# The angle of the last layer in turns, and 64-row expert blocks whose halves TensorE adds

## The chip, the cores and the metric

The kernel runs on one core of a Trainium2 chip. The metric is the device time of one execution in microseconds (us). TensorE is called PE here, its weight loads PEld, VectorE DVE, ScalarE ACT, GpSimd POOL, and SyncE, which issues most transfers, SP.

## What is computed

Three layers run one after another: attention over pooled queries, eight experts of which each routed row uses one, and a last dense layer with a cosine. The parts that the change touches are these two.

```python
for e in range(E):                                   # experts, 512 -> 1024 -> 512
    mask = e_idx == e
    h = np.maximum(xc[mask] @ w1[e], 0.0)
    y[mask] = gate_w[mask, None] * (h @ w2[e])
out[do_compute] = xc + y

h = x @ w_in                                         # last layer, 512 -> 2048 -> 512
g = h * np.cos(h)
return (g @ w_out).astype(np.float32)
```

Here x has 2304 rows. The inputs are float32, and w_out is float64 (the kernel sees it as pairs of 32-bit words).

## The kernel before

A scheduler takes the program as written and sets the order of the instructions on each engine by its own estimates; each engine then runs its queue in order. So an edit can reorder work that it does not touch.

**Split operands.** Every large product is made of three: a float32 operand is split into a rounded part and the rest (names ending in h and l), and high by high, high by low and low by high are summed in PSUM.

**Experts** (about 553 to 748 us). The rows are handled in 13 blocks of 256, 128 or 64 rows; eight of the 13 have 64. The weights come in pieces: SP issues a load into one of six buffers (stage, L696), ACT rounds it (whl, L701), and DVE makes the rest (L702). For a block of 64 rows, the input's two parts stand side by side as 128 columns, so one product gives the partial sum of the high part in PSUM partitions 0 to 63 and that of the low part in 64 to 127. mm1's function hidden adds the two: for each of two halves of 512 columns, DVE copies the lower partitions up (L747) and adds the upper ones (L748). The result hs (64 x 1024) is turned by eight 64 x 64 transposes on PE (L677 in transposed), and then ACT applies Relu and rounds (L680) and DVE makes the rest (L681). Then the second product (ops), DVE's y with gate and residual (L791, L793) and POOL's scatter to HBM follow. ORDERS gives the order in which pieces of a block's first product, the block before's second product and the transposes are written.

**Last layer** (class Ffn, from about 751 us to the end). The rows come in six chunks of 384, in three pairs, and there are 16 column steps f for each pair. A step has 24 matmuls into hp (12 for each chunk, L955) and 18 into o (9 for each chunk, L984); the o products of a chunk run five items of work (LAG) behind its hp products. While the first pair runs, the weights of each step are loaded and split too: wih and wil (L909 to L911) from wraw, and w_out in narrow(), where four DVE operations and one ACT square build float32 numbers from 64-bit words (woo, L875 to L882), then woh (L920, mostly POOL) and wol (L921, mostly DVE). Pairs two and three find the weights ready.

**The angle.** With sin² of half the angle, h·cos(h) is −2·h·(sin²−½). For each chunk and step, ACT computes t = hp/2π + MAGIC, whose addition rounds to a whole number (L958), and copies hp to h (L959). POOL takes MAGIC off again and multiplies by −C1 (L960), DVE adds h (L961), and DVE adds the small rest of 2π (L962). ACT takes the sine of half of that and squares it (L966, L967), DVE makes h = (r − ½)·h (L968), POOL rounds it (gh, L970), and DVE or POOL makes the rest (gl, L971; by the table GLP, POOL makes 11 of the first pair's 32). The factor −2 is applied to the output (L1031, L1033).

Of the kernel before, what the change touches and what calls it, by code (L numbers as in the profile page):

```python
# [634 lines left out]
class Experts:  # L635
    def __init__(self, tc, ctx, stage, early, xts, w1, w2, ident, xg, x2, lst):
        self.tc, self.nc, self.ident = tc, tc.nc, ident
        self.w1, self.w2, self.xg, self.x2, self.lst = w1, w2, xg, x2, lst
        pool = lambda name, bufs, **kw: ctx.enter_context(tc.tile_pool(name=name, bufs=bufs, **kw))
        self.stage, self.early, self.count = stage, early, 0  # L640

        self.hl0 = pool("hl0", 1)
        self.px = pool("ex1", 2)
        self.hl1 = pool("hl1", 1)
        self.p2 = pool("ex2", 2)
        self.p3 = pool("ex3", 6)
        self.psh = pool("psh", 2, space=PSUM)
        self.pst = pool("pst2", 2, space=PSUM)
        self.pso = pool("pso", 2, space=PSUM)
        self.prev, self.xts = [], xts  # L650

    def gather(self, off, rows):
        nc = self.nc
# [7 lines left out]
    def transposed(self, srcs, nch, rows, relu=False):  # L661


        nc = self.nc
        part = lambda t: (self.px if nch == 4 else self.p2).tile([128, nch, 256], F32R, name=("xT" if nch == 4 else "hT") + t, bufs=2)
        if rows == 64:
            both = part("h")
            tiles = [(both[:, :, 0:64], both[:, :, 64:128], nch)]
        else:
            both = part("h"), part("l")  # L670
            tiles = [tuple(t[:, :, 128 * b:128 * b + 128] for t in both) + (4,) for b in range(len(srcs))]
        for src, (hi, lo, n) in zip(srcs, tiles):
            for c0 in range(0, nch, n):
                tp = self.pst.tile([128, n, min(rows, 128)], F32, name="tp2")
                for c in range(n):
                    m = tp.shape[2]
                    nc.tensor.transpose(tp[:, c, :], src[0:m, (c0 + c) * 128:(c0 + c + 1) * 128], self.ident[0:m, 0:m])  # L677
                h, l = hi[:, c0:c0 + n], lo[:, c0:c0 + n]
                if relu:
                    nc.scalar.activation(h, tp, AF.Relu)  # L680
                    nc.vector.scalar_tensor_tensor(l, tp, 0.0, h.bitcast(F32), ALU.max, ALU.subtract)  # L681
                else:
                    nc.scalar.copy(h, tp)
                    nc.vector.tensor_tensor(l, tp, h.bitcast(F32), ALU.subtract)
        return both
# [26 lines left out]
    def mm1(self, group, xT, rows):  # L712
# [20 lines left out]
        def hidden():  # L733
            if rows == 256:
                hh, hl = (self.p2.tile([128, 8, 256], F32R, name="hT" + t, bufs=2) for t in "hl")
                for a in range(4):
                    p = h[a // 2][:, a % 2, :].rearrange("p (a b) -> p a b", a=2)
                    s = slice(2 * a, 2 * a + 2)
                    nc.scalar.activation(hh[:, s], p, AF.Relu)
                    nc.vector.scalar_tensor_tensor(hl[:, s], p, 0.0, hh[:, s].bitcast(F32), ALU.max, ALU.subtract)  # L740
                res.append((hh, hl))
                return
            hs = self.p2.tile([128, FF], F32, name="hs")
            for a in range(2):
                s = slice(512 * a, 512 * a + 512)
                if rows == 64:
                    nc.vector.tensor_copy(hs[0:64, s], h[0][64:128, a, :])  # L747
                    nc.vector.tensor_tensor(hs[0:64, s], h[0][0:64, a, :], hs[0:64, s], ALU.add)  # L748
                else:
                    nc.scalar.activation(hs[:, s], h[0][:, a, :], AF.Relu)  # L750
            res.append(hs)
# [134 lines left out]
class Ffn:  # L886

    MAGIC = 12582912.0
    C1 = 6.28125
    C2 = 0.0019353071795864769  # L890

    def __init__(self, tc, ctx, w_in, w_out64, ident, x2, out):
        self.tc, self.nc, self.ident, self.x2, self.out = tc, tc.nc, ident, x2, out
# [52 lines left out]
    def hidden(self, x, f, m):  # L946
# [8 lines left out]
                nc.tensor.matmul(hp, w[:, d], a[:, d], start=d + k == 0, stop=d == 3 and k == 2)  # L955
        T = lambda name, dt=F32, bufs=3: self.p3.tile([128, 384], dt, name=name, bufs=bufs)
        t, r, h = T("t", F32, TB), T("r", F32, RB), T("h", F32, HB)
        nc.scalar.activation(t, hp, AF.Identity, bias=self.magic, scale=0.15915494309189535)  # L958
        self.copied = nc.scalar.copy(h, hp)  # L959
        nc.gpsimd.tensor_scalar(t, t, -self.MAGIC, -self.C1, ALU.add, ALU.mult)  # L960
        nc.vector.tensor_tensor(r, t, h, ALU.add)  # L961
        nc.vector.scalar_tensor_tensor(r, t, self.C2 / self.C1, r, ALU.mult, ALU.add)  # L962

        def rest():
            with self.tc.issue_after(self.copied.ins):
                nc.scalar.activation(r, r, AF.Sin, scale=0.5)  # L966
                nc.scalar.activation(r, r, AF.Square)  # L967
                nc.vector.scalar_tensor_tensor(h, r, 0.5, h, ALU.subtract, ALU.mult)  # L968
                gh, gl = T("gh", F32R, LAG + 1), T("gl", F32R, LAG + 1)
# [16 lines left out]
    def run(self):  # L986
# [35 lines left out]
        def project():  # L1022
# [4 lines left out]
            if f == 15:  # L1027
                for t in range(3):
                    ot = self.p1.tile([128, DM], F32, name="fx", bufs=6)
                    if t == 1:  # L1030
                        nc.vector.tensor_scalar(ot, o[m][t], -2.0, 0.0, ALU.mult, ALU.add)  # L1031
                    else:
                        nc.scalar.mul(ot, o[m][t], -2.0)  # L1033
                    nc.sync.dma_start(self.out[384 * m + 128 * t:384 * m + 128 * t + 128, :], ot)

        for f in range(WO):
# [168 lines left out]
```

## Time and profile before

| | us |
|---|---|
| three runs | 1192.21, 1194.04, 1196.78 |
| median | 1194.04 |
| the profiled execution, its own time | 1202.32 |
| its span, first to last instruction | 1200.6 |

In the profiled execution PE is busy for 93% of the span, DVE for 79%, ACT for 65% and POOL for 49%, and the mean granted clock is 0.979 of full speed. Busy shares are averages over three layers with different limits, so the stretches have to be read one by one. Matmuls overlap, and the record's end of a matmul is modelled: the rate of PE is better read from the start of one group to the start of the next.

### The profile page before, as it was taken

What the parts mean: (1) busy time and instruction counts of PE and PEld (TensorE: products, weight loads), DVE (VectorE), ACT (ScalarE), POOL (GpSimd) and SP (SyncE); (2) the same over time, 40 slices, a digit from 0 to 9 for tenths busy, and PEclk for the clock granted to TensorE, in tenths of its full rate; (3) what the DMA queues carried; (4) which work ended last, traced back from release to release, by engine and by line L of the source; (5) the groups of instructions that cost most, each with busy time, mean ns of one, the idle gap of its engine ahead of it and who ended that gap; (6) DMA issues with size and microseconds to landing.
All of it is one profiled execution on the core that took longest, in us unless ns stands there. A gap on an engine that the chain in (4) does not pass through costs nothing. (4 is left out here: it accounts for less than half of the span.)

```text
span 1200.6 us, 20635 instructions
## 1 busy us (share of the span) xinstructions
PE 1119.4 (93%) x6722; PEld 1002.4 (83%) x6722; DVE 946.3 (79%) x1957; ACT 775.9 (65%) x2016; POOL 584.4 (49%) x828
## 2 busy tenths in 40 slices
PE   3999999999999999999999996789998999999998
PEld 2999898899888999898776874678877989898987
DVE  7989898999898999898689657698987755565554
ACT  3889898899888999897266433554444544454443
POOL 7587666776576666734412121355454332223231
PEclk9999999999999999998999998889998999999999
DMA  6575567466664566343568542532111300010001
GB/s 182 148 197 146 154 201 174 123 162 172 205 175 120 152 202 167 105 136 132 176 207 295 188 179 76 201 115 71 53 53 36 106 1 1 1 53 1 1 1 53
DMA packets 62638, 147.72 MB, mean 123 GB/s; under 512 B 17882, under 2 KB 17882, under 8 KB 62528
## 3 DMA queue, kind: packets, MB, share of 16 engines
q1 hardware_dynamic: 59840, 141.75, 40.1%
q0 software_dynamic: 2688, 4.62, 1.2%
q8 instruction: 55, 0.90, 0.3%
q14 instruction: 55, 0.45, 0.1%
HBM read 91.93 MB, written 21.69 MB: 95 GB/s over the span
## 5 line engine op out<-in xcount | busy, mean ns | idle before, releaser
L234 DVE TENSOR_REDUCE m<-s 128x1 f32<-128x384 f32 x432 | 236.8, 553 | 48.5 <-PE s L225 37.8
L243 ACT ACTIVATE p<-s,m 128x384 f32<-128x384 f32 x432 | 247.8, 583 | 21.6 <-DVE m L238 18.7
L225 PE MATMUL s<-k,qa 128*128 128x384 f32 x768 | 226.9, 379 | 34.1 <-ACT p L243 18.3
L261 PE MATMUL tp<-ident,p 128*128 128x128 f32 x1296 | 202.2, 275 | 5.0 <-DVE ptsml L277 3.2
L261 PEld LDWEIGHTS tp<-ident,p 128*128 128x128 f32 x1296 | 162.6, 142 | 18.0 <-issue 2.1
L225 PEld LDWEIGHTS s<-k,qa 128*128 128x128 f32 x768 | 119.3, 194 | 43.7 <-ACT p L243 25.8
L958 ACT ACTIVATE t<-hp,magic 128x384 f32<-128x384 f32 x96 | 55.6, 579 | 138.5 <-PE hp L955 138.5
L955 PE MATMUL hp<-fxh,wih 128*128 128x384 f32 x384 | 131.6, 343 | 8.4 <-ACT h L959 7.0
L955 PE MATMUL hp<-fxl,wih 128*128 128x384 f32 x384 | 130.3, 339 | 0.5 <-DVE fxl L942 0.5
L955 PE MATMUL hp<-fxh,wil 128*128 128x384 f32 x384 | 130.3, 339 | 0.0
L960 POOL TENSOR_SCALAR t<-t 128x384 f32<-128x384 f32 x96 | 60.5, 630 | 137.0 <-ACT t L958 134.1
L984 PE MATMUL o<-woh,gh 128*128 128x512 f32 x288 | 116.0, 403 | 3.1 <-ACT woh L918 3.1
L984 PE MATMUL o<-wol,gh 128*128 128x512 f32 x288 | 115.7, 402 | 2.0 <-DVE wol L921 2.0
L984 PE MATMUL o<-woh,gl 128*128 128x512 f32 x288 | 115.2, 400 | 0.0
L277 DVE TENSOR_TENSOR ptbigl<-tp,ptbigh 128x384 fp32r<-128x384 f32 x208 | 112.3, 544 | 0.0
L961 DVE TENSOR_TENSOR r<-t,h 128x384 f32<-128x384 f32 x96 | 68.0, 708 | 52.8 <-POOL t L960 52.3
L970 POOL TENSOR_SCALAR gh<-h 128x384 fp32r<-128x384 f32 x96 | 70.4, 746 | 77.3 <-DVE h L968 70.1
L968 DVE SCALAR_TENSOR_TENSOR h<-r,h 128x384 f32<-128x384 f32 x96 | 56.4, 622 | 58.3 <-ACT r L967 58.3
L701 ACT CAST whl<-stage 128x1024 fp32r<-128x1024 f32 x64 | 66.2, 1054 | 55.5 <-DMA stage<-w 39.8
L272 ACT CAST ptbigh<-tp 128x384 fp32r<-128x384 f32 x208 | 93.9, 491 | 10.2 <-PE tp L261 9.5
L277 DVE TENSOR_TENSOR ptsml<-tp,ptsmh 128x384 fp32r<-128x384 f32 x176 | 95.2, 546 | 1.5 <-ACT ptsmh L272 1.5
L272 ACT CAST ptsmh<-tp 128x384 fp32r<-128x384 f32 x176 | 81.4, 489 | 20.9 <-PE tp L261 14.6
(237 smaller groups left out, 2860.6 us busy)
## 6 DMA issues: line engine op xcount, KB each, us to landing
stage<-w SPq DMA_DIRECT2D x64, 512.0 KB
k<-stage SPq DMA_DIRECT2D x60, 288.0 KB
qa<-stage SPq DMA_DIRECT2D x60, 256.0 KB
stage<-v SPq DMA_DIRECT2D x16, 576.0 KB
stage<-q SPq DMA_DIRECT2D x15, 576.0 KB
stage<-k SPq DMA_DIRECT2D x15, 576.0 KB
wiw<-w_in SPq DMA_DIRECT2D x16, 512.0 KB
wow<-w_out SPq DMA_DIRECT2D x16, 512.0 KB
```

What stands on the lines that cost most here:

```text
L225: nc.tensor.matmul(o[:, 0:384], w, m[:, 384 * n:384 * n + 384], start=t == 0, stop=t == len(prods) - 1)
L234: self.last_max = nc.vector.tensor_reduce(s["m", c][:, n:n + 1], s["s", c, n][:, 0:384], AX.X, ALU.min)
L243: self.nc.scalar.activation(s["p", c][:, 384 * n:384 * n + 384], s["s", c, n][:, 0:384], AF.Exp, bias=s["m", c][:, 3:4], scale=-1.0, accum ...
L261: nc.tensor.transpose(tp[:, a, :], p[:, (3 * n + a) * 128:(3 * n + a + 1) * 128], self.ident)
L272: self.nc.scalar.copy(hi, tp)
L277: self.nc.vector.tensor_tensor(lo, tp, hi.bitcast(F32), ALU.subtract)
L701: nc.scalar.copy(hi, raw)
L955: nc.tensor.matmul(hp, w[:, d], a[:, d], start=d + k == 0, stop=d == 3 and k == 2)
L960: nc.gpsimd.tensor_scalar(t, t, -self.MAGIC, -self.C1, ALU.add, ALU.mult)
L961: nc.vector.tensor_tensor(r, t, h, ALU.add)
L970: nc.gpsimd.tensor_scalar(gh, h, 1.0, 0.0, ALU.mult, ALU.add)
L984: self.nc.tensor.matmul(o[t], a[:, s], w, start=f + k == 0, stop=f == 15 and k == 2)
```

## The change

In the experts, for blocks of 64 rows, ACT now copies hs whole, all 128 partitions, and the eight transposes become eight products of a 128 x 128 slice of hs with fold, a 128 x 64 tile of two identities one above the other; such a product turns the slice and adds its halves at once. fold is made by two POOL copies at the start of the experts. DVE's copies and additions go. In the last layer, the copy h is hp/2π, so the angle is counted in turns: one DVE operation forms (t − MAGIC) − h, POOL's operation on t and DVE's addition go, the sine's scale is π, and the output's factor is −4π.

```diff
--- before.py
+++ after.py
@@ -648,6 +648,9 @@
         self.pst = pool("pst2", 2, space=PSUM)
         self.pso = pool("pso", 2, space=PSUM)
         self.prev, self.xts = [], xts
+        self.fold = self.px.tile([128, 64], F32, name="fold", bufs=1)
+        for r in (slice(0, 64), slice(64, 128)):
+            self.nc.gpsimd.tensor_copy(self.fold[r], ident[r, r])
 
     def gather(self, off, rows):
         nc = self.nc
@@ -673,8 +676,12 @@
             for c0 in range(0, nch, n):
                 tp = self.pst.tile([128, n, min(rows, 128)], F32, name="tp2")
                 for c in range(n):
-                    m = tp.shape[2]
-                    nc.tensor.transpose(tp[:, c, :], src[0:m, (c0 + c) * 128:(c0 + c + 1) * 128], self.ident[0:m, 0:m])
+                    s, m = slice((c0 + c) * 128, (c0 + c + 1) * 128), tp.shape[2]
+                    if relu:
+
+                        nc.tensor.matmul(tp[:, c, :], src[:, s], self.fold, start=True, stop=True)
+                    else:
+                        nc.tensor.transpose(tp[:, c, :], src[0:m, s], self.ident[0:m, 0:m])
                 h, l = hi[:, c0:c0 + n], lo[:, c0:c0 + n]
                 if relu:
                     nc.scalar.activation(h, tp, AF.Relu)
@@ -744,8 +751,7 @@
             for a in range(2):
                 s = slice(512 * a, 512 * a + 512)
                 if rows == 64:
-                    nc.vector.tensor_copy(hs[0:64, s], h[0][64:128, a, :])
-                    nc.vector.tensor_tensor(hs[0:64, s], h[0][0:64, a, :], hs[0:64, s], ALU.add)
+                    nc.scalar.copy(hs[:, s], h[0][:, a, :])
                 else:
                     nc.scalar.activation(hs[:, s], h[0][:, a, :], AF.Relu)
             res.append(hs)
@@ -886,8 +892,7 @@
 class Ffn:
 
     MAGIC = 12582912.0
-    C1 = 6.28125
-    C2 = 0.0019353071795864769
+    TURN = 0.15915494309189535
 
     def __init__(self, tc, ctx, w_in, w_out64, ident, x2, out):
         self.tc, self.nc, self.ident, self.x2, self.out = tc, tc.nc, ident, x2, out
@@ -955,15 +960,13 @@
                 nc.tensor.matmul(hp, w[:, d], a[:, d], start=d + k == 0, stop=d == 3 and k == 2)
         T = lambda name, dt=F32, bufs=3: self.p3.tile([128, 384], dt, name=name, bufs=bufs)
         t, r, h = T("t", F32, TB), T("r", F32, RB), T("h", F32, HB)
-        nc.scalar.activation(t, hp, AF.Identity, bias=self.magic, scale=0.15915494309189535)
-        self.copied = nc.scalar.copy(h, hp)
-        nc.gpsimd.tensor_scalar(t, t, -self.MAGIC, -self.C1, ALU.add, ALU.mult)
-        nc.vector.tensor_tensor(r, t, h, ALU.add)
-        nc.vector.scalar_tensor_tensor(r, t, self.C2 / self.C1, r, ALU.mult, ALU.add)
+        nc.scalar.activation(t, hp, AF.Identity, bias=self.magic, scale=self.TURN)
+        self.copied = nc.scalar.mul(h, hp, self.TURN)
+        nc.vector.scalar_tensor_tensor(r, t, self.MAGIC, h, ALU.subtract, ALU.subtract)
 
         def rest():
             with self.tc.issue_after(self.copied.ins):
-                nc.scalar.activation(r, r, AF.Sin, scale=0.5)
+                nc.scalar.activation(r, r, AF.Sin, scale=np.pi)
                 nc.scalar.activation(r, r, AF.Square)
                 nc.vector.scalar_tensor_tensor(h, r, 0.5, h, ALU.subtract, ALU.mult)
                 gh, gl = T("gh", F32R, LAG + 1), T("gl", F32R, LAG + 1)
@@ -1028,9 +1031,9 @@
                 for t in range(3):
                     ot = self.p1.tile([128, DM], F32, name="fx", bufs=6)
                     if t == 1:
-                        nc.vector.tensor_scalar(ot, o[m][t], -2.0, 0.0, ALU.mult, ALU.add)
+                        nc.vector.tensor_scalar(ot, o[m][t], -4 * np.pi, 0.0, ALU.mult, ALU.add)
                     else:
-                        nc.scalar.mul(ot, o[m][t], -2.0)
+                        nc.scalar.mul(ot, o[m][t], -4 * np.pi)
                     nc.sync.dma_start(self.out[384 * m + 128 * t:384 * m + 128 * t + 128, :], ot)
 
         for f in range(WO):
```

The scheduler's order moves with it. On DVE in the first pair of the last layer, one column step reads as follows before; woo and wol are the weights of w_out, r, h and gl belong to the angle.

```order
L921 TENSOR_TENSOR wol_10939<-woo,woh_10938 128x512
L968 SCALAR_TENSOR_TENSOR h<-r,h 128x384 x2
L961 TENSOR_TENSOR r<-t,h 128x384
L971 TENSOR_TENSOR gl<-h,gh 128x384
L962 SCALAR_TENSOR_TENSOR r<-t,r 128x384
L971 TENSOR_TENSOR gl<-h,gh 128x384
L875 TENSOR_SCALAR woo<-wow 128x512
L961 TENSOR_TENSOR r<-t,h 128x384
L876 SCALAR_TENSOR_TENSOR woo<-wow,woo 128x512
L962 SCALAR_TENSOR_TENSOR r<-t,r 128x384
L877 SCALAR_TENSOR_TENSOR woo<-wow,woo 128x512
L882 SCALAR_TENSOR_TENSOR woo<-wow,woo 128x512
```

And now:

```order
L926 TENSOR_TENSOR wol_10928<-woo,woh_10927 128x512
L971 SCALAR_TENSOR_TENSOR h<-r,h 128x384 x2
L965 SCALAR_TENSOR_TENSOR r<-t,h 128x384
L974 TENSOR_TENSOR gl<-h,gh 128x384 x2
L881 TENSOR_SCALAR woo<-wow 128x512
L882 SCALAR_TENSOR_TENSOR woo<-wow,woo 128x512
L965 SCALAR_TENSOR_TENSOR r<-t,h 128x384
L883 SCALAR_TENSOR_TENSOR woo<-wow,woo 128x512
L888 SCALAR_TENSOR_TENSOR woo<-wow,woo 128x512
```

The two additions (L961) are gone, and the single operation of the angle (L965) stands where they stood; here both gl are DVE's before and now.

On ACT, at the end of the experts, the last block's rows read as follows before; whl are weight pieces being rounded, hTh is the Relu of the turned block.

```order
L701 CAST whl_10401<-stage_10399 128x1024
L680 ACTIVATE hTh<-tp_10277 128x8x64
L701 CAST whl_10410<-stage_10408 128x1024
L701 CAST whl_10419<-stage_10417 128x1024
L701 CAST whl_10428<-stage_10426 128x1024
L680 ACTIVATE hTh<-tp_10373 128x8x64
```

And now:

```order
L708 CAST whl_10388<-stage_10386 128x1024
L708 CAST whl_10397<-stage_10395 128x1024
L708 CAST whl_10406<-stage_10404 128x1024
L754 COPY hs<-hps 128x512 x2
L708 CAST whl_10415<-stage_10413 128x1024
L687 ACTIVATE hTh<-tp_10360 128x8x64
```

The two copies of hs stand behind three weight pieces and ahead of the last one.

On PE in the middle of the experts, the turning of a 64-row block (tp) stands among the matmuls of the next block's first product (hps). Before:

```order
L772 MATMUL hps<-whl_8562,xTl 128x512
L677 MATMUL tp_8998<-ident,hs 128x64 x4
L772 MATMUL hps<-whl_8562,xTh 128x512 x2
L772 MATMUL hps<-whl_8562,xTl 128x512
L772 MATMUL hps<-whl_8562,xTh 128x512
L772 MATMUL hps<-whl_8565,xTh 128x512
L677 MATMUL tp_8998<-ident,hs 128x64 x4
```

And now:

```order
L778 MATMUL hps<-whl_8562,xTl 128x512
L778 MATMUL hps<-whl_8562,xTh 128x512 x2
L682 MATMUL tp_8999<-fold,hs 128x64 x8
L778 MATMUL hps<-whl_8562,xTl 128x512
L778 MATMUL hps<-whl_8562,xTh 128x512
L778 MATMUL hps<-whl_8565,xTh 128x512
```

The turning is one piece of eight products instead of two pieces of four, and follows its block's products more closely.

## Rows read from the trace of the kernel before

**Rows 1.** Windows, first pair: stretch, us, busy (count) PE PEld DVE ACT POOL, PEclk

```profile
757.00:780.00 23.00, 19.79 (x108) 17.66 (x108) 17.66 (x29) 15.84 (x34) 10.51 (x11) 1.00 0.57 198
780.00:840.00 60.00, 52.17 (x239) 45.81 (x238) 54.76 (x77) 29.65 (x64) 33.62 (x37) 0.91 0.30 93
840.00:900.00 60.00, 57.09 (x279) 49.18 (x277) 54.57 (x84) 26.72 (x60) 29.65 (x38) 1.00 0.17 53
900.00:920.00 20.00, 14.89 (x66) 12.41 (x66) 17.62 (x26) 8.75 (x20) 11.58 (x14) 0.83 0.17 53
```

**Rows 2.** Windows of one line alone: L955 (hp) above, L984 (o) below

```profile
757.00:920.00 163.00, 78.30 (x396) 70.75 (x396) 0.95 0.28 88
...
757.00:920.00 163.00, 70.26 (x261) 50.78 (x261) 0.95 0.28 88
```

**Rows 3.** Chain that ended last: start us, us, what

```profile
871.63 0.69 DVE woo L882
...
880.68 0.69 DVE woo L882
...
935.79 4.19 PE o L984 x18
939.98 4.16 PE hp L955 x24
```

**Rows 4.** Lines of 640 to 900 by form: busy us, mean ns, idle before

```profile
L962 DVE SCALAR_TENSOR_TENSOR r<-t,r 128x384 f32<-128x384 f32 x29 | 23.8, 819 | 0.0
L960 POOL TENSOR_SCALAR t<-t 128x384 f32<-128x384 f32 x29 | 23.3, 805 | 9.4 <-ACT t L958 7.1 <-POOL gh L970 0.2
L961 DVE TENSOR_TENSOR r<-t,h 128x384 f32<-128x384 f32 x29 | 21.1, 729 | 4.2 <-POOL t L960 4.0
...
L968 DVE SCALAR_TENSOR_TENSOR h<-r,h 128x384 f32<-128x384 f32 x27 | 19.2, 741 | 1.0 <-ACT r L967 1.0
...
L971 DVE TENSOR_TENSOR gl<-h,gh 128x384 fp32r<-128x384 f32 x19 | 15.2, 800 | 0.8 <-POOL gh L970 0.8
...
L876 DVE SCALAR_TENSOR_TENSOR woo<-wow,woo 128x512 int32<-128x512 int32 x14 | 10.7, 761 | 0.1
L882 DVE SCALAR_TENSOR_TENSOR woo<-wow,woo 128x512 f32<-128x512 f32 x14 | 10.0, 711 | 1.0
...
L921 DVE TENSOR_TENSOR wol<-woo,woh 128x512 fp32r<-128x512 f32 x12 | 9.7, 806 | 8.2 <-POOL woh L920 8.2
...
L875 DVE TENSOR_SCALAR woo<-wow 128x512 int32<-128x512 int32 x14 | 8.8, 632 | 0.0
```

**Rows 5.** The same view of 850 to 1201, line L962

```profile
L962 DVE SCALAR_TENSOR_TENSOR r<-t,r 128x384 f32<-128x384 f32 x79 | 50.3, 637 | 1.0
```

**Rows 6.** Waits of PE, 757 to 920: us in total, times, longest us

```profile
PE hp L955 <- ACT h L959: 7.0, 7, 2.7
PE hp L940 <- DVE fxl L942: 3.8, 1, 3.8
```

**Rows 7.** Timeline of the last expert block: start us, us, instruction [idle before]

```profile
735.88 1.05 ACT L701 CAST whl<-stage 128x1024 fp32r<-128x1024 f32 x1 [1.51 <-SPq L1175]
...
737.97 0.46 PE L677 MATMUL tp<-ident,hs 64*128 64x64 f32 x4 [1.51 <-DVE hs L748]
...
740.61 0.80 PE L766 MATMUL ops<-whl,hTh 128*128 128x512 f32 x1 [2.18 <-DVE hTh L681]
```

**Rows 8.** Lines of the whole span by form

```profile
L329 PE MATMUL av<-sel,avs 128*128 128x73 f32 x256 | 36.8, 267 | 0.5 <-ACT avs L306 0.5
...
L747 DVE COPY hs<-hps 64x512 f32<-64x512 f32 x16 | 11.1, 693 | 3.3 <-PE hps L766 2.9
...
L677 PE MATMUL tp<-ident,hs 64*128 64x64 f32 x64 | 7.1, 234 | 2.1 <-DVE hs L748 2.0
...
L750 ACT ACTIVATE hs<-hps 128x512 f32<-128x512 f32 x4 | 2.2, 596 | 3.3 <-PE hps L772 3.3
```

**Rows 9.** Waits of ACT in the experts, 560 to 757

```profile
ACT whl L701 <- DMA stage<-w: 39.8, 19, 9.4
```

## Prediction

> **What bounds the kernel now.** I read the windows first, then the chain of work that ended last, then the lines and waits of the stretches that lose time, and the order of both kernels. The last layer's pairs two and three are at PE's rate: in the chain 24 hp products take 4.16 us and 18 o products 4.19 us, one group right behind the other [rows 3]. So a column step costs PE 8.35 us, 0.173 us for an hp product and 0.233 for an o product. From about 930 us to the end nothing but PE sets the time, and an engine relieved there gives nothing.
>
> The first pair is another matter. Between 757 and 920 us PE did 396 hp and 261 o products [rows 2]; at those rates 68.6 + 60.8 = 129.4 us, and some 4 us more for 30 transposes of inputs. The stretch is 163 us long, so about 29 us of PE's time are lost. I spread them over the stretches by their count of instructions, at 133.4/687 = 0.194 us each (the four add up to 692, as an instruction that crosses a border counts twice) [rows 1]: 780 to 840 has 239, worth 46, and loses 14; 840 to 900 has 279, worth 54, and loses 6; 900 to 920 has 66, worth 13, and loses 7; the first 23 us have 108, worth 21, and lose 2, or nearer 4 since most of those are the cheaper hp products. DVE is what stands over these: it is busy 54.76 and 54.57 of 60 us, more than 90% [rows 1], and the chain runs through its operations, with the same woo operation at 871.63 and 880.68 [rows 3]. A step takes 9.05 us there, 0.70 above PE's 8.35. PE's own waits name ACT's h for 7.0 us in seven waits and fxl, DVE's last of the next pair's inputs, for 3.8 us in one [rows 6]. ACT's h has to wait for a buffer that DVE frees, so both go back to DVE. The granted clock is 0.91 and 0.83 of full speed in the two stretches that wait most, and 1.00 in the others [rows 1].
>
> In the experts PE waits little but at the end: in the last block the second half of the transposes starts after 1.51 us of waiting for DVE's addition, and the second product after 2.18 us of waiting for DVE's rest of the Relu [rows 7].
>
> **The angle.** Per chunk and step, one POOL operation and one DVE addition go; of 96 each, 32 lie in the first pair, two a step. The DVE step in the order before has wol, two h, two additions (L961), two L962, two gl, and four woo. By the means of the stretch that is 0.81 + 1.48 + 1.46 + 1.64 + 1.60 + four times about 0.70 = 9.8 us [rows 4]. The step itself took 9.05, so the means, which take in the slow start, are 7% high. Without the additions it is 9.8 − 1.46 = 8.3, or 7.7 scaled by 9.05/9.8. I take 7.7, from the later step, and keep 8.3 for the range; the single operation that stays is of L962's form, with an immediate and one tile more, and 0.82 is counted for it. Either is below PE's 8.35, so PE becomes the bound, with little to spare: at 92 to 99% of the step DVE still holds up someone now and then. On POOL two operations of 0.81 us a step go [rows 4]; POOL is half busy (29.65 of 60 [rows 1]), so this gives little by itself, but t reaches DVE without that step between. ACT's h is a multiplication in place of a copy, of the same size, which I put at nothing: if it were as long as t's (both are one pass over 128 x 384) ACT at 26.72 of 60 us covers it.
>
> What comes back, by stretch. 840 to 900: at 7.7 the loss of 6 us falls to 1. 780 to 840: DVE's backlog from the first weights causes most of the 14; arrival of the first weights and the order of woh and wol behind them stay; I leave 3. 900 to 920: fxl stands behind a shorter queue, and the clock that falls when PE waits has less reason to; I leave 2 to 3 of 7. The start: 3 of 2 to 4 stay, since it waits for loads. Left are 9 to 10 of 29: **−20 us**, −26 if only the start stays, −13 if half of the middle stays.
>
> **The experts.** DVE loses 16 copies and 16 additions, 11.1 + 10.9 = 22 us [rows 8]; ACT gains 16 copies of 128 x 512, at the 0.596 us of the nearest row, its Relu of the same tile, 9.5 us. Neither is the bound over most of that stretch. On PE, 64 transposes had 7.1 us busy, 0.111 each. A product with fold is not in the trace. Its nearest row is the attention's float32 product with a selecting tile, L329: 256 in 36.8 us, 0.144 each with 73 columns [rows 8]. The difference is 0.033 × 64 = 2 us; I take 3, since the weights that it loads are full 128 x 128, and keep 0 to 7 (as much again as the transposes).
>
> The Trainium skill ("FP8 and Floating Point Precision", section "TensorE Precision Notes") states that true float32 takes four passes through the array. No run here shows a pass-through transpose to cost a quarter of a float32 product; L329's row stands against it. By the page, against a one-pass transpose, fold would cost 64 × 3 × 0.111 = 21 us.
>
> At the end, the chain copy, addition, transposes becomes copy, products. DVE's copy, y and addition stood between the last first-layer product and the transposes; ACT's two copies take 1.2 us. The waits of 1.51 and 2.18 us [rows 7], 3.7 together, and what shorter ones the block before has, make −4 (−1, if ACT's queue takes most of it back, to −7). In between, the copies now stand in ACT's queue among the weight pieces, and the fold products follow their block sooner: by the order, in some blocks only four products of 0.23 us lie between. I add 1 us of waits for that, and take 1 off for less DVE ahead of whl. POOL's two copies for fold come once, 64 columns each against the 384 of L960's 0.81 us, and I put them at nothing. Sum: +3 − 4 + 1 − 1 = **−1 to −3; I take −2** (−8 to +6).
>
> **Sum.** The profiled execution took 1202.32 us; −20 − 2 gives 1180.3. It lies 8.3 us above the median of the runs, and I take the same difference off the median of 1194.04: **1172 us**.
>
> **Rivals.** (a) *The step stays bound by DVE.* Its queue is in order, and each step has waits in it, for POOL's woh before wol and for the sine before h; if they stay and the step is 8.3 plus half a microsecond, the middle gains 0.25 a step, 3 us in 13 steps, and the slow start and the end of the pair some 6. For it: busy 54.57 of 60 leaves 5.4 us of waits in 6.6 steps, 0.8 a step [rows 1]; against it: a queue with room can run ahead. The first pair gains 9, the experts 2: 1183.
>
> (b) *More comes free than is counted.* L962 took 819 ns in the first pair, and 637 in the stretch from 850 on, where POOL has less to do [rows 4, 5]. If POOL's t operations stretch the DVE operations beside them, taking away two a step saves 0.2 us each besides, DVE's step is 7.3, only the start loses, and the experts' end gives 5: −26 − 5, 1163. The Trainium skill ("SBUF — State Buffer", section "Who interferes with whom") has a rule of this kind: the only contention is over a port pair that DVE and GpSimd share, as an exclusive lock. The two means agree with it; nothing here separates it from mere waiting.
>
> (c) *Slower: ACT's queue in the experts.* The copies of hs stand behind rounding of weight pieces, which waits for loads: 39.8 us in 19 waits, 2.1 on average, 9.4 at the longest [rows 9], and each piece takes 1.05 more [rows 7]. A block whose copies stand behind two such pieces starts its products 6.3 us late, and in the last block they stand behind three. Before, DVE did this work without ACT. With about 2 us of other products as cover, eight blocks lose 4.3 each, 34 us, and the time is 1194 − 20 + 34 = 1208. From 20/8 = 2.5 us of uncovered wait a block it eats the gain. Against it: the waits for loads fall where buffers are late for DVE's rest, and a relieved DVE frees buffers sooner; and the order has 4 to 36 products between a block's last first-layer product and its turning, 1 to 8 us.
>
> (d) *The products with fold cost four times the transposes*: +21 on PE in the experts, 1172 − 3 + 21 = 1190.
>
> (e) *The change doesn't do what it says*: the scheduler's estimates put other work where the additions were, and the pair stays as it is; 1192, since the experts' −2 remain.
>
> **How the numbers follow.** The forecast 0.62, (a) 0.17, (b) 0.10, (c) 0.05, (d) 0.03, (e) 0.03. The forecast's own range is the median with −13 − 2 + 6 at one end and −26 − 8 at the other, 1160 to 1185; the range for 8 in 10 leaves out (c), (d), (e) and the corners, and takes in (a): **1160 to 1187**. About 0.5%, 6 us, is what a measurement of this kernel can tell from no change. Faster by more than that (below 1188) are the forecast, (b) and nearly all of (a): 0.88; within it (d), (e) and the rest of (a): 0.07; slower (c): 0.05.
>
> **What would show it.** Right: in 840 to 900 the woo operations repeat every 8.35 to 8.5 us and the chain there is PE's; PE waits under 4 us for h and for fxl; pair one ends some 20 us sooner, and pairs two and three keep 8.35 a step. In the experts, the wait of the last second product falls below 1 us and PE's waits for hs on ACT add up to less than 3 us. Wrong: a step that still takes 8.8 us with DVE in the chain (a); ACT's hs as the releaser of long PE waits (c); 0.4 us for a product with fold (d). The prediction falls above all if something other than DVE's load held the first pair, such as the loads of w_out into their one buffer.

## The result, and the profile after

| | median, us | range | runs |
|---|---|---|---|
| before | 1194.44 | 1192.21 to 1196.78 | 4 |
| changed | 1180.66 | 1176.92 to 1183.68 | 4 |

The ratio is 0.9887 (95% interval 0.9856 to 0.9917), or −13.5 us (−9.9 to −17.2). The forecast was 1172, −22: the direction held and the time lies in the range, but four tenths of the gain are missing.

The stages, in us, from the starts of TensorE's (PE's) products in the traces: attention ends at the experts' first product; the first pair runs from its first hp product to the first of the second pair, the 385th of 1152.

| | attention | experts | to first hp | first pair | rest | span |
|---|---|---|---|---|---|---|
| before | 562.0 | 183.5 | 12.0 | 158.5 | 284.7 | 1200.6 |
| before, once more | 562.8 | 183.1 | 12.2 | 158.7 | 284.6 | 1201.4 |
| changed | 555.1 | 178.1 | 12.5 | 150.0 | 283.8 | 1179.5 |

So the first pair gave 8.5 us where 20 were forecast, and the experts 5.4 where 2 were. Together that is 13.9, about the measured 13.5; attention, whose 7 us in the profile are not in the medians, is taken up below. The rest, pairs two and three, came between 283.6 and 286.7 us in all the profiles, so differences of that size in it are not read as effects.

The page of the changed kernel, busy time and PE's granted clock:

```profile
PE 1113.0 (94%) x6786; PEld 1006.6 (85%) x6786; DVE 870.1 (74%) x1829; ACT 783.4 (66%) x2032; POOL 530.2 (45%) x734
...
PEclk9999999999999999999999999799999999999999
```

VectorE (DVE) lost 76 us of busy time. The lines that answer to [rows 4] and [rows 8], over the whole span:

```profile
L965 DVE SCALAR_TENSOR_TENSOR r<-t,h 128x384 f32<-128x384 f32 x96 | 67.3, 701 | 59.2 <-ACT h L964 59.1
...
L682 PE MATMUL tp<-fold,hs 128*128 128x64 f32 x128 | 15.3, 273 | 0.0
...
L754 ACT COPY hs<-hps 128x512 f32<-128x512 f32 x16 | 8.6, 587 | 4.6 <-PE hps L772 4.6
```

The single operation of the angle takes 701 ns. The products with fold are recorded 128 times for 64 products, 15.3 us against the transposes' 7.1. The copies on ScalarE (ACT) take 587 ns, as priced.

The first pair by stretch (length, busy us and count of PE, PEld, DVE, ACT, POOL, then PEclk), to be read beside [rows 1]:

```profile
745.00:768.00 23.00, 20.87 (x108) 19.29 (x107) 16.98 (x28) 17.35 (x37) 7.34 (x7) 0.90 0.59 198
768.00:828.00 60.00, 55.22 (x273) 48.51 (x272) 52.08 (x73) 32.54 (x70) 26.13 (x27) 1.00 0.31 95
828.00:868.00 40.00, 40.00 (x201) 35.81 (x200) 32.10 (x50) 19.43 (x44) 13.70 (x18) 1.00 0.20 62
868.00:888.00 20.00, 14.36 (x62) 12.64 (x61) 14.22 (x21) 7.00 (x16) 7.99 (x10) 0.86 0.21 61
888.00:908.00 20.00, 18.53 (x98) 15.58 (x98) 11.46 (x19) 10.97 (x25) 4.87 (x7) 0.97 0.05 19
```

At the forecast's 0.194 us an instruction, 828 to 868 holds 201, 39.0 of 40 us: PE loses almost nothing there. 868 to 888 holds 62, worth 12.0, and loses 8. The old end of the pair, 900 to 920 in [rows 1], lost 7. So the middle was mended and the end was not. PE's waits in the pair, beside [rows 6], and DVE's longest:

```profile
PE hp L960 <- ACT h L964: 10.4, 6, 4.6
...
PE hp L945 <- DVE fxl L947: 0.9, 1, 0.9
```

```profile
DVE woo L881 <- DMA wow<-w_out: 12.7, 6, 2.7
```

The wait for inputs (fxl) went from 3.8 to 0.9 us, but that for ACT's h grew from 7.0 to 10.4; and DVE, which never waited for a load of w_out before, now does so for 12.7 us. The chain shows where (start us, us, what):

```profile
858.02 3.32 DMA wow<-w_out
...
861.43 0.44 DVE woo L881
...
867.63 3.37 DMA wow<-w_out
...
871.09 0.44 DVE woo L881
```

From one load of wow to the next, 9.6 us pass, more than PE's 8.35 a step. The timeline shows what that does to PE (start us, us, instruction, idle before it):

```profile
871.09 0.43 DVE L881 TENSOR_SCALAR woo<-wow 128x512 int32<-128x512 int32 x1 [2.09 <-DMA wow<-w_out]
...
872.16 1.02 DVE L971 SCALAR_TENSOR_TENSOR h<-r,h 128x384 f32<-128x384 f32 x2
...
872.28 0.67 ACT L886 ACTIVATE wow<-wow 128x512 f32<-128x512 f32 x1 [3.93 <-DVE woo L882]
...
873.31 0.49 ACT L964 ACTIVATE h<-hp 128x384 f32<-128x384 f32 x1
...
873.85 0.45 PE L960 MATMUL hp<-fxh,wih 128*128 128x384 f32 x1 [1.02 <-ACT h L964]
...
880.48 0.43 DVE L881 TENSOR_SCALAR woo<-wow 128x512 int32<-128x512 int32 x1 [1.86 <-DMA wow<-w_out]
...
881.67 0.69 ACT L886 ACTIVATE wow<-wow 128x512 f32<-128x512 f32 x1 [2.87 <-DVE woo L882]
```

```profile
883.25 0.69 PE L960 MATMUL hp<-fxh,wih 128*128 128x384 f32 x1 [4.62 <-ACT h L964]
```

DVE stands before the first operation on w_out and waits 2.09 us for the load, until 871.09; the two h of the angle, queued behind it, start after it. From there the delay reaches PE through ACT. ACT's square of wow (L886) needs DVE's second operation on w_out (L882), and it stands in ACT's queue ahead of the t and h of the next chunk. The hp products of that chunk were done at 866.5; ACT sat idle for 3.93 us until L882 let the square start at 872.28, h followed at 873.31, and PE's next hp product, which needs the PSUM buffer that t and h read, waited 1.02 us. At 880.48 the same happens again, and at 883.25 PE has waited 4.62 us. From 882.5 to 889.3 the granted clock is at its lower level, 1.2 GHz: the twelve hp products from 883.25 on take 3.68 us from the first start to the last, where the chunk before took 2.02. These two waits are 5.6 of the 10.4 us; the other 4.8 come before 802 us, while the first weights arrive.

In the order of the changed kernel this can be seen without a trace. DVE's queue in the last full step of the pair:

```
L926 TENSOR_TENSOR wol_10938<-woo,woh_10937 128x512
L881 TENSOR_SCALAR woo<-wow 128x512
L882 SCALAR_TENSOR_TENSOR woo<-wow,woo 128x512
L883 SCALAR_TENSOR_TENSOR woo<-wow,woo 128x512
L971 SCALAR_TENSOR_TENSOR h<-r,h 128x384 x2
L965 SCALAR_TENSOR_TENSOR r<-t,h 128x384
L974 TENSOR_TENSOR gl<-h,gh 128x384
L888 SCALAR_TENSOR_TENSOR woo<-wow,woo 128x512
L965 SCALAR_TENSOR_TENSOR r<-t,h 128x384
```

In the step that was shown with the change, L881 and L882 stood behind h and gl. From step to step they climb, and here three of the four are ahead of the two h.

### The profile page after: what moved, and what is told of

Same layout as the page of the kernel before. It is cut to its first block, busy times and chain, and to the rows that moved or that the text cites. A ratio compares the mean times of both kernels' runs of the same rounds, so it can differ in the third digit from the quotient of the medians.

```text
span 1179.5 us, 20417 instructions
## 1 busy us (share of the span) xinstructions
PE 1113.0 (94%) x6786; PEld 1006.6 (85%) x6786; DVE 870.1 (74%) x1829; ACT 783.4 (66%) x2032; POOL 530.2 (45%) x734
## 3 DMA queue, kind: packets, MB, share of 16 engines
q0 software_dynamic: 2688, 4.62, 1.2%
## 5 line engine op out<-in xcount | busy, mean ns | idle before, releaser
L973 POOL TENSOR_SCALAR gh<-h 128x384 fp32r<-128x384 f32 x96 | 68.0, 722 | 268.2 <-DVE h L971 246.8
L960 PE MATMUL hp<-fxh,wih 128*128 128x384 f32 x384 | 131.5, 343 | 11.9 <-ACT h L964 10.4
L971 DVE SCALAR_TENSOR_TENSOR h<-r,h 128x384 f32<-128x384 f32 x96 | 52.6, 584 | 83.4 <-ACT r L970 83.3
L965 DVE SCALAR_TENSOR_TENSOR r<-t,h 128x384 f32<-128x384 f32 x96 | 67.3, 701 | 59.2 <-ACT h L964 59.1
L960 PEld LDWEIGHTS hp<-fxh,wih 128*128 128x128 f32 x384 | 72.9, 190 | 18.8 <-ACT h L964 13.7
L243 ACT ACTIVATION_READ_ACCUMULATOR p<-s,m 128x1 f32 x432 | 88.2, 204 | 0.0
```

The costliest lines, as they stand in the source:

```text
L243: self.nc.scalar.activation(s["p", c][:, 384 * n:384 * n + 384], s["s", c, n][:, 0:384], AF.Exp, bias=s["m", c][:, 3:4], scale=-1.0, accum ...
L965: nc.vector.scalar_tensor_tensor(r, t, self.MAGIC, h, ALU.subtract, ALU.subtract)
L973: nc.gpsimd.tensor_scalar(gh, h, 1.0, 0.0, ALU.mult, ALU.add)
```

## Experiments

Each run's expectation was written before it. A run with several rounds has a ratio; for single ones, the time of the first pair or of the experts is the measure, as the same kernel's two profiles agree in these within 0.4 us, and kernels with the same last layer within 1.2 (150.0, 151.1 and 151.2).

### The kernel before once more, and the two parts alone

The first is the kernel before with no edit, the second has the class Ffn of the change, the third all of the change but that class.

> The kernel before once more with a profile, for the spread of its parts: attention, experts and last layer took 562.0, 183.5 and 455.1 us. If the 7 us by which attention ended earlier in the profile of the changed kernel (which leaves attention as it is) are the spread of single executions, attention ends between 553 and 562 us here. If the 562 repeats within 1 us, the change moves attention too.

> The angle in turns alone, with the 64-row blocks as before. In the traces the stretch from the last product of the experts to the end took 455.1 us before and 446.3 us with the whole change, and the experts 183.5 and 178.1. Theory A (the parts are independent): this run is 8 to 10 us faster than before, its last layer takes 446 to 447 us and its experts 183 to 184. Theory B (the two parts need each other, because an earlier end of the experts starts the weights of the last layer sooner): 3 to 6 us faster, with a last layer of 449 us or more. If the prediction's sum had been right it would be 20 us faster.

> The 64-row blocks with the product with fold alone, the angle as before. Theory A: 4 to 6 us faster than before, experts 178 us, last layer 455. Theory B: the experts' gain in the trace was the profiled executions' own spread, and this is within 2 us of before. The rival of the prediction, that ACT's copies queue behind weight pieces, asks for a slower run with PE's waits naming ACT's hs.

| | ratio to before | attention | experts | first pair |
|---|---|---|---|---|
| before, once more | | 562.8 | 183.1 | 158.7 |
| angle alone | 0.9950 (0.9921 to 0.9979) | 555.5 | 183.6 | 151.2 |
| experts alone | 0.9952 (0.9931 to 0.9973) | 562.0 | 178.7 | 159.0 |

Each part gives its gain alone: −7.4 us in the pair and −4.8 in the experts, and both ratios are near −6 us, together about −12 of the −13.5. By the last layer as a whole the angle alone took 449.3 us, which is theory B's figure; but 2.0 of the 3.0 us over the changed kernel's 446.3 lie in the rest (285.8 against 283.8), within its spread. So a small part that needs both is not ruled out. ACT's queue is no trouble: hs is not among what PE's products wait for.

Attention repeats at 562 with the old angle, which by the first run's expectation would mean that the change moves attention; and it came between 552.0 and 558.9 in all the profiles with the new angle, though its instructions stand in the same order. Yet the angle alone is only 6 us faster by its runs (2.5 to 9.5), which the pair's 7.4 use up. So these 7 us don't show in the runs' medians. The clock goes with a part of them: within attention, PE was at half clock for 13.7 us in both profiles of the kernel before and for 3.6 in that of the changed one, and 10 us at half the rate cost about 5, an estimate. But two profiles with 10.2 us at half clock took 562.0 (experts alone) and 555.3 (the order held, below), so the rest stays open.

### The load of w_out: read earlier, and two buffers

First guess: the loop through the one buffer of wow is the bound. The first run moves the square's result out of wow, so that wow comes free earlier; the second gives wow two buffers, and makes room by writing the angle into t; the third has that room-making alone.

```diff
-    nc.scalar.activation(m, m, AF.Square)
+    nc.scalar.activation(sq, m, AF.Square)          # sq: the tile of woh
```

```diff
-    raw = pool.tile([128, n, 2], I32, name=tag + "w", bufs=1)
+    raw = pool.tile([128, n, 2], I32, name=tag + "w", bufs=2 if tag == "wo" else 1)
...
-TB, RB, HB, WB, XB = (4, 2, 4, 2, 2)
+TB, RB, HB, WB, XB = (3, 2, 4, 2, 2)
...
-        t, r, h = T("t", F32, TB), T("r", F32, RB), T("h", F32, HB)
+        t, h = T("t", F32, TB), T("h", F32, HB)
+        r = t
```

> The whole change, and in the preparation of w_out ACT's square goes to the tile that later holds woh instead of back into wow, so that wow is read for the last time two DVE operations earlier and its next load can be issued earlier. Theory A (the end of the first pair is bound by the loop of the one buffer wow: load 3.4 us, then four DVE operations with others between, 9.6 us in all against PE's 8.35): the loop shrinks to 8.4 us or less, the wait of DVE for wow falls from 12.7 us to 6 or less, and the run is 3 to 8 us faster than the changed kernel, 1173 to 1177. Theory B (DVE's own work is the bound and the wait for wow only fills its slack): within 2 us of the changed kernel.

> The whole change, with two buffers for wow; the room for it is made by writing the angle into the tile of t (no tile r) and by three of those instead of four. The first pair, from its first hp product to the first of the second pair, took 158.5 and 158.7 us in two profiles of before, 150.0 in the changed kernel. Theory A (after the change the load of w_out into one buffer, for which DVE waits in order, holds the end of the first pair): DVE's wait for wow falls from 12.7 us to under 3, the pair takes 142 to 146 us, the run is 4 to 8 us faster than the changed kernel. Theory B (the loads are not the bound; the pair's rest loss is the start and the inputs of the second pair): the pair takes 148 to 151 us.

> The control for the run with two buffers: the angle is written into the tile of t, three of them, and wow keeps its one buffer. If only the buffer counts, the pair takes 149 to 152 us as in the changed kernel; if the tiles count, it moves with the run with two buffers.

| | ratio | first pair |
|---|---|---|
| square aside | 0.9882 (0.9857 to 0.9906) | 150.6 |
| two buffers | 0.9885 (0.9858 to 0.9912) | 150.6 |
| room-making alone | 0.9862 (0.9831 to 0.9892) | 146.1 |

This theory fell. With the square aside, DVE's wait for wow falls to 8.7 us only, and ACT now waits for the load, too, in its queue, where the square still stands ahead of t and h (us in total, times, longest):

```profile
ACT woh L887 <- DMA wow<-w_out: 34.8, 13, 4.5
```

With two buffers, DVE's wait for wow's load is gone altogether, and still PE waits longer for ACT's h than in the changed kernel:

```profile
PE hp L960 <- ACT h L965: 15.3, 9, 3.1
```

There, too, ACT's square waits for L882 (up to 6.0 us) ahead of most of the late h, though no load is waited for. The control without the second buffer, which still waits 9.0 us for wow, is 4.5 us faster in the pair, outside what was expected either way. DVE's order differs in all of these (in the control, too, operations on w_out stand ahead of the h of a step). So these runs say that a second buffer doesn't mend the end of the pair, and not yet what does.

### DVE's and POOL's operation, one at a time

In the first run DVE has a second operation for the angle again, in the second GpSimd (POOL) has its operation on t again.

```diff
         nc.vector.scalar_tensor_tensor(r, t, self.MAGIC, h, ALU.subtract, ALU.subtract)
+        nc.vector.tensor_scalar(r, r, 1.0, 0.0, ALU.mult, ALU.add)
```

```diff
-        nc.vector.scalar_tensor_tensor(r, t, self.MAGIC, h, ALU.subtract, ALU.subtract)
+        nc.gpsimd.tensor_scalar(t, t, 1.0, -self.MAGIC, ALU.mult, ALU.add)
+        nc.vector.scalar_tensor_tensor(r, t, 0.0, h, ALU.subtract, ALU.subtract)
```

> The whole change, and DVE copies r onto itself after the angle, so that DVE has two operations for an angle again, and POOL none. The prediction said that DVE's load is what held the first pair. Theory A (DVE's load): the pair takes 155 to 159 us, as before the change. Theory B (POOL's operation and its place between ACT and DVE was what cost): the pair stays at 149 to 152 us.

> The whole change, but POOL takes MAGIC off t as before and DVE's one operation subtracts h: POOL's operation is back, DVE's second is not. Theory A (DVE's load): the pair takes 150 to 153 us, hardly more than in the changed kernel. Theory B (POOL's operation): 155 to 159 us.

The pair took 144.5 us with DVE's second operation and 160.7 with POOL's. More work for DVE made the pair 5.5 us *faster*, which is outside both theories (160.7 is just above theory B's range). The order of the first run points to why: with that operation in, the scheduler leaves L881 behind h, r and gl in every steady step, as in the kernel before. Two things are mixed here, work and order, and the next runs part them.

### The order held

Now one thing is held: the first of the four operations on w_out is queued behind the last h written before it. Nothing else in the program changes.

```diff
+    with after():                                   # self.tc.issue_after(self.turned.ins), from the second step on
-    v.tensor_scalar(o, top, 3, 0x3FFFFFF8, ALU.logical_shift_left, ALU.bitwise_and)
+        v.tensor_scalar(o, top, 3, 0x3FFFFFF8, ALU.logical_shift_left, ALU.bitwise_and)
...
-                nc.vector.scalar_tensor_tensor(h, r, 0.5, h, ALU.subtract, ALU.mult)
+                self.turned = nc.vector.scalar_tensor_tensor(h, r, 0.5, h, ALU.subtract, ALU.mult)
```

The second run has POOL's operation back besides, as above. In the third, which is the run with two DVE operations, POOL copies t onto itself when DVE has read it, so that it works beside DVE and nobody waits for it soon:

```diff
         nc.vector.tensor_scalar(r, r, 1.0, 0.0, ALU.mult, ALU.add)
+        nc.gpsimd.tensor_scalar(t, t, 1.0, 0.0, ALU.mult, ALU.add)
```

> The whole change, with one thing held: the first of the four DVE operations that prepare w_out is queued behind the last h = (r - 1/2)h written before it. In the changed kernel the scheduler puts it, and in the end the two after it, ahead of the two h of its step; with this it stands behind h, r and gl in every step, as before the change. Theory A (the order: DVE waits in order for wow's load while the angle's work behind it is ready): the first pair takes 143 to 147 us against 150.0, PE's waits on ACT's h fall from 10.4 us to under 6, the run is 3 to 7 us faster than the changed kernel (ratio to before about 0.983). Theory B (the order doesn't matter, one slow load does): 149 to 151 us.

> The run with POOL's operation back and one DVE operation for an angle (160.7 us), with the first operation on w_out held behind h as in the run above. Theory A (the order made most of its 160.7): 147 to 152 us. Theory B (POOL's operation makes it): 156 us or more.

> The run with two DVE operations for an angle (whose pair took 144.5 us), and POOL's operation on t is back, but behind the angle and beside it: it copies t onto itself when DVE has read it, and nobody waits for it but the next use of the tile. DVE's order is that of the run with two DVE operations. Theory A (POOL's operation takes time from DVE's operations beside it): the pair takes 154 to 159 us, and the means of DVE's operations rise as they stood before, h from 0.58 to 0.70 us. Theory B (POOL's operation cost only as a link in the chain from ACT to DVE): 144 to 147 us.

With the order held, the change runs at 1173.81 us (1169.98 to 1179.66; six runs), ratio 0.9835 (0.9807 to 0.9863), and the pair takes 139.4 us. It is faster than the kernel before; through that kernel it stands 0.9835/0.9887 = 0.995 to the changed one, about 6 us, though the two intervals overlap at the edge. The pair is shorter than theory A had it (143 to 147). Its first pair by stretch, and PE's wait for ACT's h in it:

```profile
745.00:770.00 25.00, 22.21 (x114) 20.49 (x115) 17.83 (x30) 17.72 (x38) 7.37 (x7) 0.90 0.61 202
770.00:830.00 60.00, 55.03 (x273) 48.53 (x272) 54.11 (x75) 32.81 (x70) 27.46 (x29) 1.00 0.33 101
830.00:880.00 50.00, 50.00 (x253) 45.19 (x252) 42.80 (x66) 26.33 (x56) 18.44 (x23) 1.00 0.22 64
880.00:900.00 20.00, 19.46 (x107) 16.72 (x106) 12.36 (x22) 11.28 (x25) 6.79 (x8) 1.00 0.09 26
```

```profile
PE hp L962 <- ACT h L966: 5.1, 4, 2.7
```

Its clock is 1.00 to the pair's end, and 880 to 900, the stretch with the second pair's inputs, holds 107 instructions where the changed kernel's worst stretch of 20 us held 62. DVE doesn't wait for wow any more, and no wait of PE for ACT's h comes after 803 us: the 5.6 us at the end are gone, and the wait at the start is as it was. In the 10.6 us by which the pair got shorter, the clock has a share: PE was at half clock for 10.5 us of the pair in the changed kernel and for 3.0 with the order held, which comes to some 4 us, an estimate by the 3.68 against 2.02 above. And not all 10.6 reach the run: in the same two profiles the experts took 1.3 us longer and the rest 2.6, and the runs give about 6. The pair in all combinations:

| POOL's operation | DVE's operations for an angle | first operation on w_out | first pair |
|---|---|---|---|
| in the chain | 2 | behind h (before) | 158.5 |
| beside | 2 | behind h | 153.6 |
| none | 2 | behind h | 144.5 |
| in the chain | 1 | held behind h | 145.1 |
| none | 1 | held behind h | 139.4 |
| in the chain | 1 | free | 160.7 |
| none | 1 | free (changed) | 150.0 |

Each line but those of the kernel before and the changed one is a single profile. In the two runs with a second DVE copy, the last step's first operation on w_out still comes ahead of its h, and DVE waits 3.4 and 3.3 us for wow there. In like order, DVE's operation is worth 13.4 us (158.5 to 145.1), POOL's 14.0 (158.5 to 144.5), both together 19.1; POOL's is worth 5.7 when DVE's is gone already. The free order costs 10.6 with POOL's operation gone, and 15.6 with it.

POOL's operation costs the pair even where nobody waits for it: beside the angle it is 9.1 us (144.5 to 153.6, just short of theory A's 154). DVE's lines in that stretch, first without it and then with it:

```profile
L965 DVE SCALAR_TENSOR_TENSOR r<-t,h 128x384 f32<-128x384 f32 x27 | 19.1, 709 | 0.0
L966 DVE TENSOR_SCALAR r<-r 128x384 f32<-128x384 f32 x27 | 17.6, 650 | 0.0
L972 DVE SCALAR_TENSOR_TENSOR h<-r,h 128x384 f32<-128x384 f32 x26 | 14.1, 582 | 1.2 <-ACT r L971 1.2
L975 DVE TENSOR_TENSOR gl<-h,gh 128x384 fp32r<-128x384 f32 x18 | 14.0, 777 | 0.4 <-POOL gh L974 0.4
```

```profile
L966 DVE TENSOR_SCALAR r<-r 128x384 f32<-128x384 f32 x25 | 20.8, 833 | 0.0
L965 DVE SCALAR_TENSOR_TENSOR r<-t,h 128x384 f32<-128x384 f32 x25 | 19.5, 782 | 0.0
L973 DVE SCALAR_TENSOR_TENSOR h<-r,h 128x384 f32<-128x384 f32 x25 | 15.0, 637 | 0.8 <-ACT r L972 0.8
L976 DVE TENSOR_TENSOR gl<-h,gh 128x384 fp32r<-128x384 f32 x18 | 13.5, 749 | 0.8 <-POOL gh L975 0.8
```

With POOL beside, the copy of r goes from 650 to 833 ns, the angle from 709 to 782, and h from 582 to 637. Over 27, 27 and 26 operations, that is 4.9 + 2.0 + 1.4 = 8.3 us of DVE's time, about what the pair lost. DVE's four lines on w_out moved both ways (L881 from 553 to 646 ns, L882 from 763 to 708). The remaining 4.9 us up to 158.5 fall to POOL's place in the chain or to the other form of DVE's operations in the kernel before; these runs don't part the two.

The Trainium skill ("SBUF — State Buffer", section "Who interferes with whom") says that DVE and GpSimd share one pair of ports as an exclusive lock. The longer means of these three agree with it; gl, which also reads two tiles of SBUF, did not get longer (777 and 749 ns), so the trace doesn't bear it out for each operation.

### Who copies hs

```diff
-                    nc.scalar.copy(hs[:, s], h[0][:, a, :])
+                    nc.vector.tensor_copy(hs[:, s], h[0][:, a, :])
```

> The whole change, but DVE instead of ACT copies hs (two copies of 128 x 512 a block, so that DVE still loses the two additions). The experts took 183.3 us before and 178.1 with the change. Theory A (the gain is the shorter chain of a block, and DVE's relief): the experts take 179 to 182 us, the wait of ACT for weight loads between 20 and 40 us. Theory B (ACT's queue delays the copies, DVE would be better): 177 us or less.

The experts took 178.0 us, as with ACT's copies (178.1), between both theories; ACT waited 28.7 us for weight loads, within theory A's 20 to 40. So neither ACT's queue nor the choice of the engine counts. What the two kernels share, addition by PE without DVE's two additions, makes the gain. By the count of products done, the changed kernel is level with the one before through most of the experts (0.4 us ahead at the 640th of 784 recorded products, 0.6 behind at the 720th), and all of the 5.4 us come in the last blocks. There the timeline answers to [rows 7]:

```profile
725.06 1.07 ACT L754 COPY hs<-hps 128x512 f32<-128x512 f32 x2
...
725.70 2.00 PE L682 MATMUL tp<-fold,hs 128*128 128x64 f32 x16
...
729.61 0.50 PE L772 MATMUL ops<-whl,hTh 128*128 128x512 f32 x1 [0.98 <-DVE hTh L688]
```

ACT's copies start at 725.06, the first fold product follows 0.64 us later with no idle time of PE before it, and the second product waits 0.98 us in place of 2.18. The kernel before ran two stretches at half clock in there, 167.8 and 178.1 us after the experts' start, 3.4 us each; the changed one has its next one only at 180.7, when its products are done. At half the rate, these 6.8 us cost about 3.4 of the 5.4 (an estimate). Whether the shorter chain of a block kept the clock up, or both came about apart, no run shows.

## Why the prediction was right, and where it was not

**What bounds the kernel.** Right: pairs two and three gave nothing (283.8 against 284.7), and the first pair held most of what there was to gain.

**DVE's load in the pair.** Wrong for the kernel as built. The forecast left 9 to 10 of 29 us and gave −20; the pair gave −8.5, and 19.1 only with the order held. Even that agreement is luck in part: the forecast put all of it down to DVE, whose operation is worth 13.4 by itself, and POOL's, which it put at little, brings the rest. The step that failed is the reading of the order: one step in the middle was taken to stand for all. The last steps, in the same listing, have two or three of L881 to L883 ahead of the two h. The prediction said that it would fall if the load of w_out held the pair; after the change the loop through the one buffer was there, with its 9.6 us, but two buffers didn't mend it and the order did. Of the rivals, (a) gave 1183, nearer than the forecast: waits in DVE's ordered queue did hold the pair, but for the load of wow, and not for woh and the sine in every step; the middle ran at PE's rate. (e), at 0.03, had the scheduler's order in it, but an unchanged pair.

The prediction also said that ACT's h waits for a buffer that DVE frees. In the kernel before, between 757 and 920 us, ACT waited 0.6 us for that, and far longer with its square of wow, ahead of t and h:

```profile
ACT wow L880 <- DVE woo L876: 68.1, 15, 5.9
```

Three of PE's seven waits for ACT's h, 1.5 of the 7.0 us, follow such a square. So where DVE made PE wait for ACT's h, it did so through ACT's queue. This is read from the traces; no run took the square from in front of t and h.

**POOL's operation "gives little by itself".** Wrong: 14.0 us by itself in like order, 9.1 even outside the chain, and still 5.7 behind the saving on DVE. The case for it was in [rows 4, 5], 819 against 637 ns, and stood only in rival (b). The two do not add up, as 19.1 is less than 13.4 and 14.0: once either is gone, PE's 8.35 us a step are the bound for most of the pair.

**End of the pair.** Forecast 2 to 3 of 7 us left; 8 were lost between 868 and 888. Same cause, by the order.

**Experts.** The tail was forecast at −4 and gave all of −5.4. The fold product was priced at +3 (0 to 7) and took 15.3 − 7.1 = 8.2 us, outside its bounds. The failing step was the division: L329's 256 records were taken for 256 products, but a float32 product leaves two records, so 0.288 us was the price of one, as fold's 0.239 shows. From start to start, a block's eight fold products hold PE for 1.70 us and its eight transposes, in two groups of four, for 0.78: 7.4 us more in eight blocks, a factor of 2.2. Rival (d) gave 21 us. The Trainium skill ("FP8 and Floating Point Precision", section "TensorE Precision Notes") states that true float32 takes four passes through the array. Inside a group the trace comes near that: fold products start 0.223 us apart, transposes 0.062, a factor of 3.6. But 0.111 us, which the 21 were worked out from, takes in the end of each group of transposes, and the prediction's L329 row, read with two records to a product, did not stand against the rule. The 8.2 us cost nothing in the sum, since the middle of the experts stayed level. ACT's wait for loads there fell from [rows 9] to this:

```profile
ACT whl L708 <- DMA stage<-w: 20.4, 12, 9.3
```

Whether that relief is what paid for fold's products was not parted; with DVE's copies the wait was 28.7 us and the experts took the same time, so 8 us of it were worth nothing.

**ACT's queue, rival (c).** Fell: no product of PE waits for hs on ACT, and DVE's copies are no better.

**The two misses offset each other in part**: −8.5 − 5.4 against −20 − 2. The pair's −8.5 lies outside the −13 to −26 that the forecast allowed it, so the time is in the range by the room that the range had left for the experts and for (a).

## What to carry to other kernels

When an edit takes work from an engine whose order a scheduler sets, read the new order over the whole stretch, the end above all: what is free to climb may come to stand in front of work that is ready, and an engine that runs in order then waits for a load while that work waits for it. Follow the delay through the other queues, too: here it reached PE by an operation of ACT that stood ahead of the work that PE needed. A single ordering edge was worth 10.6 us of the pair and about 6 of the run here, more than the buffers that seemed to be short. And price an operation of one engine by what it does to its neighbour's durations, too: compare the same line's mean in a stretch where the neighbour works and in one where it rests.

## What the runs showed of the hardware

A float32 product that adds (fold, 128 x 64) leaves two records and takes 0.239 us of PE's busy time, one of the old transposes (64*128, 64x64) one record and 0.111; inside a group they start 0.223 and 0.062 us apart. DVE's copy of a 128 x 384 tile onto itself takes 650 ns, and 833 with one more POOL operation beside each angle. During a wait of 4.62 us by PE the granted clock fell from 2.4 to 1.2 GHz for 6.8 us, and twelve products took 3.68 us from first start to last in place of 2.02.
